# Token combinations of the first large block on VectorE instead of GpSimd, one per row tile, in an attention kernel with two feed-forward layers

## Chip, cores and metric

One core of a Trainium2 chip runs the whole program. The metric is device microseconds of one execution. A value is the median of several runs.

## What is computed

An attention over 4 x 8 heads of 576 tokens (a local one and one on tokens averaged by four) gives 2304 tokens of 512 features. Two feed-forward layers follow:

```python
def _moe_ref(x, w_in, w_out, s, b):
    h = x @ w_in                  # 512 -> 2048
    r = np.maximum(h, 0.0)
    g = s * (r * r) + b
    return (g @ w_out)            # 2048 -> 512

def _moe2_ref(x, w_in, w_out):
    h = x @ w_in
    g = h - np.tanh(h)
    return (g @ w_out)
```

All is fp32. The kernel splits each matrix operand into a rounded high part and a low part (names ending in h and l) and adds three products: high by high, high by low, low by high.

## The kernel before, in words

The second layer works on blocks of tokens, `SIZES2 = (256, 512, 512, 512, 512)`. The first, of 256 tokens, is the **plain block**. The other four are taken in two pairs, the **large blocks** (`k_` is 0 and 1), by seven products in place of eight (`wino`): sums and differences of weight pieces (`A11`, `S2`, ...) are multiplied by sums and differences of token pieces (`B11`, `T1`, `T2`, `B21`, `T3`, `T4`, `B22`).

The plain block runs over 16 **row tiles** `i`. Each has 12 matmuls for `x @ w_in` (`l1`, into the PSUM tile `ph`, two buffers), then `act2`: tanh on ScalarE into `th`, a difference on VectorE, a rounding cast to `gh` on ScalarE, and the rest `gl` on VectorE, which frees `ph`. Two tiles later come six matmuls for `g @ w_out` (`l2_2`, into `acc`). In between, the last weights are made from raw words (`w_split`: `wraw` to `wf` to `w`, on ScalarE and VectorE; `sf` are sums of weight pieces), and the tokens of the first large block are prepared: `x_load` fetches four pieces into `xr`; `x_ops` makes four differences (`comb`, the **combinations** T1 to T4) and splits all seven pieces into `xo` (`split`: cast on ScalarE, rest `xol` on GpSimd); `w1_split` rounds the first weights of the large block into `w1r`. Then `wino` begins: its products go to PSUM tiles `wb`, first with `w1r`, and later rows of `g` meet weights from the ring `w2r`. `wb` takes the PSUM buffers of `ph`, so the first ones wait for the last `gl`.

The order on each engine comes from a list scheduler at the end of the program (`list_schedule`). Of the instructions that are ready by its own estimates it takes the one of lowest priority number, and numbers rise in the order in which the code is written. `ahead(n)` lowers the number by n. Each engine then works strictly in its order, waiting at every instruction until its inputs and its buffer are there.

In `x_ops` the engine is an argument; for the first pair it is GpSimd, for the second VectorE:

```python
    XENG = (pool, dve)
    ...
            todo = x_ops(XENG[0])
        if i == 9:
            x_place()
            for f in todo:
                f()
```

Of the kernel before, what the change touches and what calls it, by code (L numbers as in the profile page):

```python
# [7 lines left out]
F32 = mybir.dt.float32  # L8
F32R = mybir.dt.float32r
I32, U32, U16 = mybir.dt.int32, mybir.dt.uint32, mybir.dt.uint16  # L10
AF = mybir.ActivationFunctionType
ALU = mybir.AluOpType
# [9 lines left out]
W2_RING = 5  # L22
NB2 = 12
Y0_AT = 6
KC = DM // 128
NF = DFF // 128
NP = NF // 2
# [55 lines left out]
def attention_moe_moe_kernel(ctx: ExitStack, tc, q, k, v, w_in, w_out, s_in, b_in, w2_in, w2_out, out):  # L83
    nc = tc.nc
    pe, act, dve, pool, sp = nc.tensor, nc.scalar, nc.vector, nc.gpsimd, nc.sync
# [12 lines left out]
    d_b = [dram.tile([128, 1024], F32, tag=f"db{i}", name="keep_b") for i in range(NB2)]  # L98
    ydram = [dram.tile([128, KC, NB1], F32, tag=f"y{u}", name=f"y{u}") for u in range(NU)]

    @contextmanager
    def ahead(n):

        tc.cur_priority = tc.cur_priority - n
        yield
        tc.cur_priority = tc.cur_priority + n
# [4 lines left out]
    scal = sb.tile([128, 2], F32, name="scal")  # L111
    bcol = sb.tile([128, KC], F32, name="bcol")

# [30 lines left out]
    def x_tiles(u):  # L144
        n = u if u < 2 else (u + 1) % 2
        X[u] = [x_p.tile([128, KC, NB1], F32R, tag=f"{t}{n}", name=t) for t in ("xh", "xl")]

# [619 lines left out]
    def l1(ph, p_, xh, xl, i):  # L767
        g, c = i // 4, (i % 4) * 128
        n = 0
        for kc in range(KC):  # L770
            w_h, w_l = wh[ph, "A", g, kc][:, c:c + 128], wl[ph, "A", g, kc][:, c:c + 128]
            x_h, x_l = (xh[kc], xl[kc]) if ph else (xh[:, kc], xl[:, kc])
            for w_, x_ in ((w_h, x_h), (w_h, x_l), (w_l, x_h)):
                pe.matmul(p_, w_, x_, start=n == 0, stop=n == 3 * KC - 1)  # L774
                n += 1
# [80 lines left out]
    def w2_step(slot):  # L856
        while w2s["n"] < NW and w2s["n"] / W2_RATE <= slot:
            n = w2s["n"]
            w_load(1, n)
            w_split(1, n)  # L860
            w2s["n"] += 1
# [83 lines left out]
    def place(items, a, b, how):  # L945
        for n, l_ in enumerate(how(items, b - a)):
            at[a + n] += l_
# [13 lines left out]
    for s_, (n, u, i) in enumerate(seq):  # L961
# [10 lines left out]
        p_ = ps_ph.tile([128, NB1], F32, tag="ph", name="ph")  # L972
# [14 lines left out]
        if s_ == HA - 1:  # L987
# [4 lines left out]
            raw_p = st1.enter_context(tc.tile_pool(name="raw", bufs=2, reuse_waits="tile"))  # L992
        if u == NU - 1 and i == Y0_AT:
            y0.append(fin.tile([128, KC, SIZES2[0]], F32, tag="yf", name="yf"))
            for e in range(2):
# [8 lines left out]
    evac1(NU - 1, None)  # L1004


    XENG = (pool, dve)

    def place(n, shape, dt, name):
        return fin.tile(shape, dt, tag=f"w{n}", name=name) if n < NFIN else sb.tile(shape, dt, tag=f"w{n - NFIN}", name=name)  # L1010
# [11 lines left out]
    def act2(i, p_):  # L1022
        t = fin2.tile([128, SIZES2[0]], F32, tag="th", name="th")
        gh = g_p.tile([128, SIZES2[0]], F32R, tag="gh", name="gh")
        gl = g_p.tile([128, SIZES2[0]], F32R, tag="gl", name="gl")
        act.activation(out=t, in_=p_, func=AF.Tanh)
        dve.tensor_tensor(out=p_, in0=p_, in1=t, op=ALU.subtract)
        act.copy(out=gh, in_=p_)
        dve.tensor_tensor(out=gl, in0=p_, in1=gh.bitcast(F32), op=ALU.subtract)
        gt[0, i] = (gh, gl)  # L1030

    def l2_2(j, i, w_, ts=None):
        gh, gl = gt[j, i]
        w_h, w_l = w_
        for t in range(SIZES2[j] // 128) if ts is None else ts:
            a_, l_ = gh[:, 128 * t:128 * t + 128], gl[:, 128 * t:128 * t + 128]
            for n, (g_, x_) in enumerate(((a_, w_h), (a_, w_l), (l_, w_h))):
                pe.matmul(accs[j][t], g_, x_, start=i == 0 and n == 0, stop=i == NF - 1 and n == 2)  # L1038
# [26 lines left out]
    ost = {}  # L1065
    w1f = []
    xo, xr, w1r, w2r, tmp, gT = {}, {}, {}, {}, {}, {}
    XOPS = ("B11", "T1", "T2", "B21", "T4", "T3", "B22")
    RAWS = ("B11", "B12", "B22", "B21", "T1", "T2", "T3", "T4")
    AT_X = (*range(40, 44), *range(10))  # L1070

    def x_place():
        for n, o in enumerate(XOPS):
            xo[o] = [place(AT_X[2 * n + i], [128, 2, 512], F32R, "xo" + "hl"[i]) for i in range(2)]

    def x_load(k_):
        for n, o in enumerate(RAWS):
            xr[o] = place(32 + n, [128, 2, 512], F32, "xr")
        for o, j, e in (("B11", 0, 0), ("B12", 1, 0), ("B22", 1, 1), ("B21", 0, 1)):
            load_y(1 + 2 * k_ + j, e, xr[o])  # L1080

    def x_ops(eng):
        def comb(o, a, b):
            return lambda: eng.tensor_tensor(out=xr[o], in0=xr[a], in1=xr[b], op=ALU.subtract)

        def split(o):
            def f():
                h, l = xo[o]
                act.copy(out=h, in_=xr[o])
                eng.tensor_tensor(out=l, in0=xr[o], in1=h.bitcast(F32), op=ALU.subtract)  # L1090
            return f
        return [comb("T1", "B12", "B11"), split("B11"), comb("T2", "B22", "T1"), split("T1"), comb("T4", "B21", "T2"),
                split("T2"), split("B21"), comb("T3", "B22", "B12"), split("T4"), split("T3"), split("B22")]

    def w1_place():
        for q_ in range(2):
            w1r[q_] = [place(32 + 4 * q_ + n, [128, 2, 512], F32R, "w1r") for n in range(4)]

    def w1_load(q_):
        if q_ >= 2 * NP:  # L1100
            return
        if not w1f:
            w1f.extend(place(10 + n, [128, 2, 512], F32, "w1f") for n in range(2))
        g, a = q_ % NP // 2, q_ % 2
        for c in range(2):
            sp.dma_start(out=w1f[0][:, c], in_=d_a[g, c, a])
            sp.dma_start(out=w1f[1][:, c], in_=d_s[g, c][a])

    def w1_split(q_):
        t = w1r[q_ % 2]  # L1110
        for n in range(2):
            act.copy(out=t[2 * n], in_=w1f[n])  # L1112
            dve.tensor_tensor(out=t[2 * n + 1], in0=w1f[n], in1=t[2 * n].bitcast(F32), op=ALU.subtract)
# [8 lines left out]
    def w2_place():  # L1122
        for n in range(W2_RING):
            w2r[n] = place(12 + n, [128, 1024], F32R, "w2r")

    def w2_fetch(m):
        if m < 4 * NB2:
            sp.dma_start(out=w2r[m % W2_RING].bitcast(F32), in_=d_b[m % NB2])
# [77 lines left out]
    def l2_row(j, i, ts=None):  # L1206
        l2_2(j, i, w2_use(j, i), ts)
        if ts is None or ts[-1] == 3:
            if i < NB2:
                w2_fetch(NB2 * (j - 1) + i + W2_RING)  # L1210
# [4 lines left out]
    for i in range(NF):  # L1215
        p_ = ps_ph.tile([128, SIZES2[0]], F32, tag="ph", name="ph2")
        l1(1, p_, ys[0], ys[1], i)
        act2(i, p_)
        if i >= LAG:
            l2_2(0, i - LAG, w_b(i - LAG))  # L1220
        w2_step(NF * NU + i - W2_SLOT0)
        if i == 0:
            x_load(0)
            todo = x_ops(XENG[0])
        if i == 9:
            x_place()
            for f in todo:
                f()
            w1_load(0)
            w1_place()  # L1230
            for q_ in range(2):
                w1_split(q_)
                w1_load(q_ + 1)
        if i == 13:
            w2_place()
            for n in range(W2_RING):
                w2_fetch(n)
    tmp_place()

    for k_ in range(2):  # L1240
        j = 1 + 2 * k_
        for p_ in range(NP):
            def fill(n):
                if p_:
                    l2_row(j, 2 * p_ - 2 + min(n, 1), (None, [0, 1], [2, 3])[n])
                elif n < 2:
                    if k_:
                        l2_row(j - 1, NF - 2 + n)
                    else:
                        l2_2(0, NF - 2 + n, w_b(NF - 2 + n))  # L1250
                else:
                    evac2(j - 1)
                    accs[j] = banks(k_ == 0)
            wino(k_, p_, fill)
        for i in range(2):
            cast(j + 1, i, gT[i // 2][:, i % 2])
            l2_row(j, NF - 2 + i)
        evac2(j)
        accs[j + 1] = banks(k_ == 1)
        if k_ == 0:  # L1260
            x_load(1)
            todo = x_ops(XENG[1])
        for i in range(2, NF):
            cast(j + 1, i, gT[i // 2][:, i % 2])
            l2_row(j + 1, i - 2)
            if k_ == 0:
                for f in todo[3 * i - 6:3 * i - 3]:
                    f()
                if i == 7:
                    w1_place()  # L1270
                    for q_ in range(NP, NP + 2):
                        w1_split(q_)
                        w1_load(q_ + 1)

# [330 lines left out]
```

## Time and profile before

| | |
|---|---|
| median of 3 runs | 963.03 us (962.78 to 963.73) |
| profiled execution | 964.05 us, span of its instructions 962.0 us |
| TensorE busy | 922.8 us, 96% of the span |
| VectorE busy | 731.8 us, 76% |
| ScalarE busy | 504.1 us, 52% |
| GpSimd busy | 181.2 us, 19% |
| mean granted TensorE clock | 0.954 of full |

The span runs from the first to the last instruction; the execution's own time is 2.05 us more. Busy TensorE means that a matmul is in flight, at whichever clock was granted. The plain block begins at 563.8 us of the span.

### The profile page before, as it was taken

To read this page: it belongs to the slowest core of one execution; us is meant where nothing else is said; L and a number is where in the kernel's file an instruction comes from. 1 tells how busy PE (TensorE), PEld (TensorE's weight loads), DVE (VectorE), ACT (ScalarE), POOL (GpSimd) and SP (SyncE) were. 2 spreads that over 40 slices of the span, in tenths; PEclk is the share of its full clock that TensorE was granted. 3 is DMA by queue.
4 is the path that set the end of the run, shared out by engine and by line. 5 is a ranking of instruction groups with operands and counts; after the bars stand their busy time and mean duration, and the time that the engine had idled before them with its cause. 6 is when DMAs were issued, how large, how long until landed. Compare 5 with 4: busy or idle time off the path is not lost.

```text
span 962.0 us, 15484 instructions
## 1 busy us (share of the span) xinstructions
PE 922.8 (96%) x5690; PEld 825.4 (86%) x5690; DVE 731.8 (76%) x1145; ACT 504.1 (52%) x1270; POOL 181.2 (19%) x139
## 2 busy tenths in 40 slices
PE   7999999969999999998999999599999999999998
PEld 6888999959999999998999999478888888888886
DVE  4567899899899999998977785987677737776621
ACT  4679654534746565464676766244434524343321
POOL 1444342432412313232200005600000000000000
PEclk7559999988999999999999999799999999999999
DMA  9991052443123132301159969154354653433061
GB/s 221 307 335 43 26 162 67 130 127 114 37 83 109 61 116 79 98 19 41 47 206 360 366 215 363 73 194 156 110 159 126 221 173 110 166 127 103 24 195 44
DMA packets 82354, 137.38 MB, mean 143 GB/s; under 512 B 23415, under 2 KB 49255, under 8 KB 82279
## 3 DMA queue, kind: packets, MB, share of 16 engines
q1 hardware_dynamic: 80662, 134.04, 42.7%
q10 hardware_dynamic: 1616, 2.36, 0.8%
q8 instruction: 45, 0.74, 0.3%
q14 instruction: 31, 0.25, 0.1%
HBM read 111.66 MB, written 24.71 MB: 142 GB/s over the span
## 4 chain that ended last, share of the span: by engine, by line
PE 74%; DVE 11%; ACT 8%; issue 3%; DMA 2%; SPq 2%; DVEq 0%; ACTq 0%
PE acc L1038 19%; PE ph L774 17%; PE wb L1179 15%; PE acc L807 14%; ACT pA L253 2%; PE S L583 2%; DVE s L194 2%; DVE xq L322 1%; PE O L606 1%; DVE pD L189 1%; SPq L510 1%; ACT E L409 1%; PE warm L892 1%; DVE gl L795 1%; DVE O L265 1%
## 5 line engine op out<-in xcount | busy, mean ns | idle before, releaser
L774 PE MATMUL ph<-xh,w 128*128 128x288 f32 x1024 | 235.5, 304 | 2.5 <-DVE gl L795 1.9
L807 PE MATMUL acc<-gh,w 128*128 128x288 f32 (+1 forms) x1024 | 227.7, 298 | 1.5 <-DVE yst L830 0.9
L774 PEld LDWEIGHTS ph<-xh,w 128*128 128x128 f32 x1024 | 174.2, 192 | 8.8 <-DVE gl L795 3.8
L807 PEld LDWEIGHTS acc<-gh,w 128*128 128x128 f32 x1024 | 171.4, 189 | 3.0 <-issue 1.7
L774 PE MATMUL ph<-xl,w 128*128 128x288 f32 x512 | 154.4, 302 | 0.1
L807 PE MATMUL acc<-gl,w 128*128 128x288 f32 x512 | 151.3, 296 | 0.7 <-DVE gl L795 0.7
L1179 PE MATMUL wb<-xoh,w1r 128*128 128x512 f32 x448 | 147.9, 395 | 0.7 <-ACT w1r L1112 0.7
L1038 PE MATMUL acc<-w2r,gx 128*128 128x512 f32 x576 | 137.2, 390 | 0.0
L1038 PEld LDWEIGHTS acc<-w2r,gx 128*128 128x128 f32 x576 | 108.1, 188 | 23.3
L786 ACT ACTIVATE ph<-ph 128x288 f32<-128x288 f32 x128 | 50.9, 398 | 105.5 <-PE ph L774 102.1
L1179 PEld LDWEIGHTS wb<-xoh,w1r 128*128 128x128 f32 x448 | 84.4, 189 | 21.3 <-ACT w1r L1112 1.1
L774 PEld LDWEIGHTS ph<-xl,w 128*128 128x128 f32 x512 | 98.0, 191 | 1.4 <-issue 0.6
L807 PEld LDWEIGHTS acc<-gl,w 128*128 128x128 f32 x512 | 96.7, 189 | 1.5 <-DVE gl L795 0.9
L1179 PE MATMUL wb<-xol,w1r 128*128 128x512 f32 x224 | 88.6, 395 | 0.0
L795 DVE TENSOR_TENSOR gl<-ph,gh 128x288 fp32r<-128x288 f32 x128 | 57.8, 452 | 29.8 <-ACT gh L792 28.9
L253 ACT ACTIVATE pA<-V,a 128x64 f32<-128x64 f32 x198 | 54.0, 342 | 9.8 <-DVE a L242 6.1
L1173 DVE TENSOR_TENSOR u<-wb,u 128x512 f32<-128x512 f32 x64 | 43.9, 687 | 15.7 <-PE wb L1179 15.7
L792 ACT CAST gh<-ph 128x288 fp32r<-128x288 f32 x128 | 50.8, 398 | 6.3 <-PE acc L807 3.1
L752 DVE SCALAR_TENSOR_TENSOR wf<-wraw 128x512 int32<-128x512 int32 x64 | 50.2, 799 | 3.7 <-ACT wraw L706 2.9
L787 ACT ACTIVATE ph<-ph 128x288 f32<-128x288 f32 x128 | 50.9, 398 | 2.4
L1165 DVE TENSOR_TENSOR gx<-gT,gx 128x512 fp32r<-128x512 f32 x32 | 22.1, 690 | 38.8 <-ACT gx L1164 38.6
L1179 PEld LDWEIGHTS wb<-xol,w1r 128*128 128x128 f32 x224 | 42.2, 189 | 9.8
(169 smaller groups left out, 1602.0 us busy)
## 6 DMA issues: line engine op xcount, KB each, us to landing
w2r<-keep_b SPq DMA_DIRECT2D x48, 512.0 KB
wraw<-in_moe_w_in_dram SPq DMA_DIRECT2D x32, 512.0 KB
wraw<-in_moe_w_out_dram SPq DMA_DIRECT2D x32, 512.0 KB
w1f<-keep_a SPq DMA_DIRECT2D x32, 256.0 KB
w1f<-keep_s SPq DMA_DIRECT2D x32, 256.0 KB
keep_b<-w SPq DMA_DIRECT2D x12, 512.0 KB
y<-yst SPq DMA_DIRECT2D x36, 144.0 KB
K<-in_k_dram SPq DMA_DIRECT2D x5, 960.0 KB
```

The lines of the kernel that those rows point to most:

```text
L253: act.activation(out=p_[:, t, h], in_=Vt[u][:, h, o + t], func=AF.Copy, scale=st["a"][:, h * TAU + t, o:o + 1])
L752: dve.scalar_tensor_tensor(out=f, in0=hw, scalar=3, in1=lw, op0=ALU.logical_shift_left, op1=ALU.bitwise_or)
L774: pe.matmul(p_, w_, x_, start=n == 0, stop=n == 3 * KC - 1)
L786: act.activation(out=p_, in_=p_, func=AF.Relu)
L787: act.activation(out=p_, in_=p_, func=AF.Square)
L792: act.copy(out=gh[:, :NB1], in_=p_)
L795: dve.tensor_tensor(out=gl, in0=p_, in1=gh[:, :NB1].bitcast(F32), op=ALU.subtract)
L807: pe.matmul(accs[u][e][:, :g_.shape[1]], w_, g_, start=i == first and n == 0, stop=i == last and n == 2)
L1038: pe.matmul(accs[j][t], g_, x_, start=i == 0 and n == 0, stop=i == NF - 1 and n == 2)
L1165: dve.tensor_tensor(out=t[:, 1], in0=g_, in1=t[:, 0].bitcast(F32), op=ALU.subtract)
L1173: add = lambda o, x, y: dve.tensor_tensor(out=o, in0=x, in1=y, op=ALU.add)
L1179: pe.matmul(b_, w1_op(q_, o, kc, i), xo[x][m][:, kc], start=n == 0, stop=n == 5)
```

## The change

The eleven elementwise operations that GpSimd did for the first large block (four combinations, seven rests `xol`) are given to VectorE. They are no longer written all at row tile 9 but one per tile from tile 5 (`X_AT`) on. The order of T3 and T4 changes, the buffers of `xr` are numbered so that the first half of `w1r` needs only four of the pieces to be used up, and each half of `w1r` is placed and written separately. `act2` of the plain block is written with a priority that is 60 ahead.

```diff
+P_ACT2 = 60
...
-    XENG = (pool, dve)
+    X_AT = 5
...
-    XOPS = ("B11", "T1", "T2", "B21", "T4", "T3", "B22")
-    RAWS = ("B11", "B12", "B22", "B21", "T1", "T2", "T3", "T4")
+    XOPS = ("B11", "T1", "T2", "B21", "T3", "T4", "B22")
+    RAWS = ("B11", "B12", "T1", "T2", "B22", "B21", "T3", "T4")
...
-    def x_ops(eng):
+    def x_ops():
         def comb(o, a, b):
-            return lambda: eng.tensor_tensor(out=xr[o], in0=xr[a], in1=xr[b], op=ALU.subtract)
+            return lambda: dve.tensor_tensor(out=xr[o], in0=xr[a], in1=xr[b], op=ALU.subtract)
...
                 act.copy(out=h, in_=xr[o])
-                eng.tensor_tensor(out=l, in0=xr[o], in1=h.bitcast(F32), op=ALU.subtract)
+                dve.tensor_tensor(out=l, in0=xr[o], in1=h.bitcast(F32), op=ALU.subtract)
             return f
-        return [comb("T1", "B12", "B11"), split("B11"), comb("T2", "B22", "T1"), split("T1"), comb("T4", "B21", "T2"),
-                split("T2"), split("B21"), comb("T3", "B22", "B12"), split("T4"), split("T3"), split("B22")]
+        return [comb("T1", "B12", "B11"), split("B11"), comb("T3", "B22", "B12"), comb("T2", "B22", "T1"), split("T1"),
+                comb("T4", "B21", "T2"), split("T2"), split("B21"), split("T3"), split("T4"), split("B22")]
...
-        act2(i, p_)
+        with ahead(P_ACT2):
+            act2(i, p_)
...
-            todo = x_ops(XENG[0])
-        if i == 9:
-            x_place()
-            for f in todo:
+            todo = x_ops()
+        if i >= X_AT:
+            for f in todo[i - X_AT:i - X_AT + 1]:
                 f()
+        if i == X_AT + 7:
             w1_load(0)
-            w1_place()
-            for q_ in range(2):
-                w1_split(q_)
-                w1_load(q_ + 1)
+            w1_place(0)
+            w1_split(0)
+            w1_load(1)
+        if i == min(X_AT + 11, NF - 1):
+            w1_place(1)
+            w1_split(1)
+            w1_load(2)
```

GpSimd's list loses its last eleven instructions and nothing else; it has no work left in the second layer. How the scheduler's order moves is seen at two places. On VectorE, behind the weight sums `sf_7174` of row tile 8, before (`ph2` and `gl` numbered 7560, 7648 and 7674 are tiles 9, 10 and 11; `wraw_7342` is the first of the last four raw weights):

```order
L732 TENSOR_TENSOR sf_7174<-wf_7128,sf_7174 128x2x128
L1027 TENSOR_TENSOR ph2_7560<-ph2_7560,th_7573 128x256
L1029 TENSOR_TENSOR gl_7575<-ph2_7560,gh_7574 128x256
L1027 TENSOR_TENSOR ph2_7648<-ph2_7648,th_7661 128x256
L708 TENSOR_SCALAR wraw_7342<-wraw_7342 128x512
L1029 TENSOR_TENSOR gl_7663<-ph2_7648,gh_7662 128x256
L752 SCALAR_TENSOR_TENSOR wf_7346<-wraw_7342 128x512
```

and now (tiles 9, 10 and 11 are 7567, 7597 and 7624):

```order
L733 TENSOR_TENSOR sf_7174<-wf_7128,sf_7174 128x2x128
L1090 TENSOR_TENSOR xol_7510<-xr_7302,xoh_7509 128x1024
L1028 TENSOR_TENSOR ph2_7567<-ph2_7567,th_7580 128x256
L1081 TENSOR_TENSOR xr_7304<-xr_7303,xr_7302 128x1024
L1030 TENSOR_TENSOR gl_7582<-ph2_7567,gh_7581 128x256
L1081 TENSOR_TENSOR xr_7308<-xr_7306,xr_7303 128x1024
L1028 TENSOR_TENSOR ph2_7597<-ph2_7597,th_7610 128x256
L1081 TENSOR_TENSOR xr_7305<-xr_7306,xr_7304 128x1024
L1030 TENSOR_TENSOR gl_7612<-ph2_7597,gh_7611 128x256
L1090 TENSOR_TENSOR xol_7594<-xr_7304,xoh_7593 128x1024
L1028 TENSOR_TENSOR ph2_7624<-ph2_7624,th_7637 128x256
L709 TENSOR_SCALAR wraw_7342<-wraw_7342 128x512
```

One combination or rest stands between every two steps of the row tiles, from tile 9 on.

The second place is where the plain block passes into the large one. On ScalarE, before (`gh_7776` and `gh_7802` are tiles 14 and 15, `w1r_7624` is the first high part of `w1r`):

```order
L1026 ACTIVATE th_7775<-ph2_7762 128x256
L706 ACTIVATE wraw_7447<-wraw_7447 128x512
L1089 CAST xoh_7594<-xr_7309 128x1024
L1028 CAST gh_7776<-ph2_7762 128x256
L1112 CAST w1r_7624<-w1f_7618 128x1024
L1026 ACTIVATE th_7801<-ph2_7788 128x256
L757 CAST w_7453<-wf_7451 128x512
L1028 CAST gh_7802<-ph2_7788 128x256
```

and now (tiles 14 and 15 are 7756 and 7786, `w1r_7690` and `w1r_7692` the high parts of the first half of `w1r`):

```order
L1027 ACTIVATE th_7755<-ph2_7742 128x256
L758 CAST w_7418<-wf_7416 128x512
L1111 CAST w1r_7690<-w1f_7684 128x1024
L758 CAST w_7453<-wf_7451 128x512
L1029 CAST gh_7756<-ph2_7742 128x256
L1111 CAST w1r_7692<-w1f_7685 128x1024
L1027 ACTIVATE th_7785<-ph2_7772 128x256
L1029 CAST gh_7786<-ph2_7772 128x256
```

The cast `gh` of tile 14 now stands behind three casts of weights, where a step on raw weights and one cast of tokens stood. On VectorE, before, from the last row tile's difference on:

```order
L1027 TENSOR_TENSOR ph2_7788<-ph2_7788,th_7801 128x256
L760 TENSOR_TENSOR w_7453<-wf_7451,w_7453 128x512
L1029 TENSOR_TENSOR gl_7803<-ph2_7788,gh_7802 128x256
L1113 TENSOR_TENSOR w1r_7625<-w1f_7618,w1r_7624 128x1024
L1050 COPY ost_7903<-acc_7265 128x512
```

and now, from tile 14's on:

```order
L1028 TENSOR_TENSOR ph2_7742<-ph2_7742,th_7755 128x256
L761 TENSOR_TENSOR w_7418<-wf_7416,w_7418 128x512
L1090 TENSOR_TENSOR xol_7681<-xr_7307,xoh_7680 128x1024
L761 TENSOR_TENSOR w_7453<-wf_7451,w_7453 128x512
L1030 TENSOR_TENSOR gl_7757<-ph2_7742,gh_7756 128x256
L1112 TENSOR_TENSOR w1r_7691<-w1f_7684,w1r_7690 128x1024
L1028 TENSOR_TENSOR ph2_7772<-ph2_7772,th_7785 128x256
L1112 TENSOR_TENSOR w1r_7693<-w1f_7685,w1r_7692 128x1024
L1030 TENSOR_TENSOR gl_7787<-ph2_7772,gh_7786 128x256
L1090 TENSOR_TENSOR xol_7729<-xr_7308,xoh_7728 128x1024
L1172 TENSOR_TENSOR u2_7815<-wb_7828,p1_7814 128x512
```

Two weight rests and one token rest now stand ahead of the `gl` of tile 14 and two rests of `w1r` ahead of that of tile 15; three token rests follow behind it, the fourth a little later. Before, the token rests were GpSimd's and the rests of `w1r` came after the last `gl`. On TensorE the order is the same up to row tile 12; the same 192 + 96 + 60 matmuls of the plain block and of `wb` stand ahead of the first one with `w2r` in both programs.

## Rows read from the trace of the kernel before

**Rows 1.** The page: span, and the granted clock in 40 slices (24.05 us each).

```profile
span 962.0 us, 15484 instructions
...
PEclk7559999988999999999999999799999999999999
```

**Rows 2.** Windows: stretch, its length, each engine's busy time, clock, DMA share, GB/s.

```profile
588.70:603.00 14.30, 14.30 (x94) 12.90 (x93) 7.61 (x13) 10.10 (x18) 14.24 (x6) 1.00 1.04 404
...
604.79:630.00 25.21, 13.11 (x45) 10.07 (x46) 19.77 (x20) 8.46 (x15) 11.88 (x5) 0.73 0.20 72
...
640.67:962.00 321.33, 317.08 (x1381) 258.50 (x1379) 200.78 (x276) 120.13 (x179) 0.00 (x0) 1.00 0.41 134
```

**Rows 3.** Timeline of TensorE: start, duration, instruction, [idle before <-releaser].

```profile
587.67 0.28 PE L774 MATMUL ph<-yxh,w 128*128 128x256 f32 x1
...
590.50 0.28 PE L774 MATMUL ph<-yxh,w 128*128 128x256 f32 x1
...
610.71 1.22 PE L1038 MATMUL acc<-w,gh 128*128 128x512 f32 x2 [5.93 <-ACT gh L1028]
...
622.55 2.07 PE L1038 MATMUL acc<-w,gh 128*128 128x512 f32 x4 [5.49 <-ACT gh L1028]
...
629.40 0.50 PE L1179 MATMUL wb<-xoh,w1r 128*128 128x512 f32 x1 [0.68 <-ACT w1r L1112]
...
630.20 0.40 PE L1179 MATMUL wb<-xol,w1r 128*128 128x512 f32 x1
...
630.90 0.62 PE L1179 MATMUL wb<-xoh,w1r 128*128 128x512 f32 x2
...
640.67 2.90 PE L1038 MATMUL acc<-w2r,gx 128*128 128x512 f32 x12
```

**Rows 4.** Timeline of ScalarE.

```profile
607.06 0.58 ACT L757 CAST w<-wf 128x512 fp32r<-128x512 f32 x1 [5.54 <-DVE wf L752]
...
628.30 2.00 ACT L1112 CAST w1r<-w1f 128x1024 fp32r<-128x1024 f32 x2
```

**Rows 5.** Timeline of VectorE in the plain block.

```profile
588.24 0.42 DVE L732 TENSOR_TENSOR sf<-wf,sf 128x256 f32<-128x256 f32 x1
...
600.33 0.42 DVE L1029 TENSOR_TENSOR gl<-ph,gh 128x256 fp32r<-128x256 f32 x1 [0.73 <-ACT gh L1028]
600.67 3.46 DVE L708 TENSOR_SCALAR wraw<-wraw 128x512 int32<-128x512 int32 x2
604.05 5.72 DVE L752 SCALAR_TENSOR_TENSOR wf<-wraw 128x512 int32<-128x512 int32 x2
...
613.09 4.70 DVE L732 TENSOR_TENSOR sf<-wf 128x256 f32<-128x256 f32 x2
```

**Rows 6.** Timeline of GpSimd.

```profile
588.76 2.41 POOL L1090 TENSOR_TENSOR xol<-xr,xoh 128x1024 fp32r<-128x1024 f32 x1 [111.25 <-DMA xr<-y]
...
598.89 2.40 POOL L1090 TENSOR_TENSOR xol<-xr,xoh 128x1024 fp32r<-128x1024 f32 x1
...
603.80 5.40 POOL L1090 TENSOR_TENSOR xol<-xr,xoh 128x1024 fp32r<-128x1024 f32 x2
612.52 7.46 POOL L1090 TENSOR_TENSOR xol<-xr,xoh 128x1024 fp32r<-128x1024 f32 x3 [3.31 <-ACT xoh L1089]
```

**Rows 7.** Timeline of VectorE in the second pair's preparation.

```profile
752.77 1.22 DVE L1084 TENSOR_TENSOR xr<-xr 128x1024 f32<-128x1024 f32 x1
753.91 0.69 DVE L1165 TENSOR_TENSOR gx<-gT,gx 128x512 fp32r<-128x512 f32 x1
754.51 1.22 DVE L1090 TENSOR_TENSOR xol<-xr,xoh 128x1024 fp32r<-128x1024 f32 x1
...
789.96 0.69 DVE L1173 TENSOR_TENSOR u<-wb,p 128x512 f32<-128x512 f32 x1 [6.92 <-PE wb L1179]
```

**Rows 8.** TensorE's timeline and a window behind an earlier, shorter wait.

```profile
436.25 0.31 PE L435 MATMUL PT<-ident,E 72*72 72x72 f32 x1 [2.53 <-DVE E L423]
...
436.20:439.00 2.80, 2.75 (x13) 2.72 (x14) 2.80 (x5) 1.19 (x3) 1.49 (x1) 0.50 0.83 249
```

More of the change, by code (lines that the diff above doesn't have):

```diff
@@ L1067, in attention_moe_moe_kernel @@
     xo, xr, w1r, w2r, tmp, gT = {}, {}, {}, {}, {}, {}
-    XOPS = ("B11", "T1", "T2", "B21", "T4", "T3", "B22")
-    RAWS = ("B11", "B12", "B22", "B21", "T1", "T2", "T3", "T4")
+    XOPS = ("B11", "T1", "T2", "B21", "T3", "T4", "B22")
+    RAWS = ("B11", "B12", "T1", "T2", "B22", "B21", "T3", "T4")
     AT_X = (*range(40, 44), *range(10))
-    def x_place():
-        for n, o in enumerate(XOPS):
-            xo[o] = [place(AT_X[2 * n + i], [128, 2, 512], F32R, "xo" + "hl"[i]) for i in range(2)]
     def x_load(k_):
@@ L1080, in x_load, with w1_place @@
             load_y(1 + 2 * k_ + j, e, xr[o])
-    def x_ops(eng):
+    def x_ops():
         def comb(o, a, b):
-            return lambda: eng.tensor_tensor(out=xr[o], in0=xr[a], in1=xr[b], op=ALU.subtract)
+            return lambda: dve.tensor_tensor(out=xr[o], in0=xr[a], in1=xr[b], op=ALU.subtract)
         def split(o):
             def f():
+                if o not in xo:
+                    n = 2 * XOPS.index(o)
+                    xo[o] = [place(AT_X[n + i], [128, 2, 512], F32R, "xo" + "hl"[i]) for i in range(2)]
                 h, l = xo[o]
                 act.copy(out=h, in_=xr[o])
-                eng.tensor_tensor(out=l, in0=xr[o], in1=h.bitcast(F32), op=ALU.subtract)
+                dve.tensor_tensor(out=l, in0=xr[o], in1=h.bitcast(F32), op=ALU.subtract)
             return f
-        return [comb("T1", "B12", "B11"), split("B11"), comb("T2", "B22", "T1"), split("T1"), comb("T4", "B21", "T2"),
-                split("T2"), split("B21"), comb("T3", "B22", "B12"), split("T4"), split("T3"), split("B22")]
-    def w1_place():
-        for q_ in range(2):
-            w1r[q_] = [place(32 + 4 * q_ + n, [128, 2, 512], F32R, "w1r") for n in range(4)]
+        return [comb("T1", "B12", "B11"), split("B11"), comb("T3", "B22", "B12"), comb("T2", "B22", "T1"), split("T1"),
+                comb("T4", "B21", "T2"), split("T2"), split("B21"), split("T3"), split("T4"), split("B22")]
+    def w1_place(q_):
+        w1r[q_] = [place(32 + 4 * q_ + n, [128, 2, 512], F32R, "w1r") for n in range(4)]
     def w1_load(q_):
@@ L1223, in attention_moe_moe_kernel @@
             x_load(0)
-            todo = x_ops(XENG[0])
-        if i == 9:
-            x_place()
-            for f in todo:
+            todo = x_ops()
+        if i >= X_AT:
+            for f in todo[i - X_AT:i - X_AT + 1]:
                 f()
+        if i == X_AT + 7:
             w1_load(0)
-            w1_place()
-            for q_ in range(2):
-                w1_split(q_)
-                w1_load(q_ + 1)
+            w1_place(0)
[5 more added lines that the diff above has]
+            w1_load(2)
         if i == 13:
@@ L1261, in attention_moe_moe_kernel @@
             x_load(1)
-            todo = x_ops(XENG[1])
+            todo = x_ops()
         for i in range(2, NF):
@@ L1269, in attention_moe_moe_kernel @@
                 if i == 7:
-                    w1_place()
                     for q_ in range(NP, NP + 2):
+                        w1_place(q_ % 2)
                         w1_split(q_)
```

## Prediction

> **What bounds the kernel now.** I read the page first, for the stretches where TensorE is not at full clock: of its 40 slices the one from 601 to 625 us shows 7 tenths, in a kernel that is otherwise at 9 nearly throughout behind the start [rows 1]. Then windows around that place. TensorE is busy for all of 588.7 to 603, but for only 13.1 of the 25.2 us from 604.8 to 630, and there at 0.73 of the clock; from 640.7 to the end it is busy for 317 of 321 us at clock 1.00 [rows 2]. So a stall between 604 and 630 is on the path, and what is won there is carried to the end unshortened.
>
> TensorE's timeline names the stall: waits of 5.93, 5.49 and 0.68 us for casts of ScalarE, 12.1 us in all [rows 3]. ScalarE was not the cause: it had itself waited 5.54 us for the `wf` of VectorE [rows 4]. VectorE was busy all that time, but with what should be short: two operations of line 708 took 3.46 us and two of line 752 took 5.72, and later two sums of line 732 took 4.70, while the `gl` at 600.33, which reads PSUM, took its 0.42 [rows 5]. A sum of line 732 at 588.24, ahead of GpSimd's first operation, took 0.42 too. What is present only in the long cases is GpSimd, at work on the token pieces from 588.76 on, 2.4 to 2.7 us for each operation [rows 6], also over that `gl`: VectorE's operations that read SBUF alone wait for it, the row tile's steps stand behind them in VectorE's order, ScalarE waits for those, and TensorE for ScalarE.
>
> **The term that is removed.** I count the TensorE work from the first matmul of row tile 9 (587.67) to the first one with `w2r` (640.67), which both programs reach after the same matmuls. A row tile of 12 + 6 matmuls takes 590.50 - 587.67 = 2.83 us [rows 3]. Seven of them (tiles 9 to 15, with the `l2` of 7 to 13) are 19.8 us. Twelve matmuls of `l2` (tiles 14, 15) and 60 of `wb` remain; three start-to-start steps of `wb` from 630.20 to 630.90 give 0.233 us each [rows 3], so 72 are 16.8 us. Together 36.6, and without any stall the `w2r` row would start at 624.3. It starts at 640.67, so 16.4 us are lost: 12.1 in waits and, by difference, 4.3 to the lower clock behind them. That is the most that the change can win in this stretch.
>
> **The term that is added.** Eleven operations of 128 x 1024 come to VectorE. Its own rows for the second pair, where GpSimd has nothing to do, give their price: 1.22 us, and 752.77 to 753.91, that is 1.14 from start to start, for a combination; a rest `xol` has the same 1.22 [rows 7]. So 12.5 us of VectorE, in a stretch where it was busy 7.6 of 14.3 us before [rows 2]; GpSimd's shared time no longer lengthens the rest. The question is when VectorE is through with what TensorE needs at the hand-over. I add up its new order from 588.66 (the end of the sum at 588.24) with start-to-start steps: 0.34 for an operation of 0.42 (600.33 to 600.67) [rows 5], 0.60 for one of 0.69 (753.91 to 754.51) [rows 7], 1.14 as above.
>
> - Up to the `wf` of the third of the last four weights: seven token operations (8.0), five differences and five `gl` (3.4), four of line 709 (1.4), three `wf` (1.8), two weight rests (1.2), four sums (1.4): 17.2, so 605.9. ScalarE then has that weight's cast, one of `w1r` and one more weight (0.5 + 1.0 + 0.5, from 0.58 and 2.00 for two [rows 4]) ahead of the `gh` of tile 14, which ends at 608.3. A clean TensorE needs it at 587.67 + 19.8 = 607.5. Gap 0.85.
> - To the `gl` of tile 14: one more `wf`, a difference, two weight rests, one `xol`, the `gl`: 3.6, so 609.5. The first product needs its PSUM buffer; TensorE is there after four matmuls, at 609.25. Gap 0.3.
> - To the `gl` of tile 15: two rests of `w1r`, a difference, the `gl`: 3.0, so 612.5. The third product needs it; TensorE is there at 613.3. No gap.
> - To the second half of `w1r`: three `xol` (3.4), eight steps of the large block (4.8), a rest of `w1r`, a step, a rest (2.9): 623.6. TensorE, late by 1.2 so far, wants the last of these at about 623.3. Gap 0.3.
>
> That is 1.5 us if VectorE never waits for ScalarE and a release costs nothing. It can only be more; for these waits I add 0.9, and take 2.4. The bounds: 0 at one end (some of the gaps close if an estimate is a little high), and at the other the waits that the same steps show when they miss each other, treated as a rival below.
>
> Other edits. The priority of `act2` and the order T3, T4 act through the orders summed above and cost nothing of their own. The same matmuls, casts and transfers are issued; SyncE's list differs only from the refills of `w1f` on, which come earlier with the rests that free them. In the second pair the preparation is written in the new order too; there the `wino` stage that it feeds shows VectorE idle for 6.92 us, waiting for TensorE, before its first step at 789.96 [rows 7], more than 30 us behind the combinations, so a shift of a few operations stays hidden. Without that cover a late piece would cost TensorE its lateness, a few times 1.14 us.
>
> **Sum.** 16.4 - 2.4 = 14.0 us less. The profiled execution took 964.05 us, 2.05 more than its span of 962.0; less 14.0 that is 950.0. It stands 1.0 above the median of the runs, so the median should be 963.0 - 14.0 = **949.0**.
>
> **A rule against the change.** The trace shows VectorE with idle time before 603 and, by the sum above, with none from there to the hand-over. The Trainium skill (Perfetto Trace Analysis, Optimizing Scalar/DVE Operations) says that with VectorE saturated, moving work to ScalarE or even GpSimd may pay, and warns that VectorE and GpSimd share an SBUF read port, so a move between those two might not. Its first half makes the first rival of what follows, and the sum by it would be that rival's; its warning is what the rows of 3.46 and 5.72 us look like.
>
> **Rivals.**
>
> *VectorE becomes the bound at the hand-over.* The gaps add up, and one grows long. For it: the sum leaves VectorE no slack from 603 to 623. Against it: the steps that TensorE waits for have priority, and by the count its largest gap is 0.85. Price: a wait of 2.53 us elsewhere left the matmuls at half the clock over 436.2 to 439.0 and to about 439.4 [rows 8], some 3.2 us at half rate, 1.6 lost. With such a gap (2.5 + 1.6) beside my 2.4 the new loss is 6.5, the gain 9.9, the time 953.1.
>
> *The low clock stays, and the kernel is slower.* If TensorE drops to 1.2 GHz at the first gap and the small gaps keep it there up to the `w2r` row, the 21.3 us of clean work left at 603 take twice as long: 21.3 + 2.4 = 23.7 lost against 16.4 now, so 7.3 slower, 970.3. It decides from (16.4 - 2.4) / 21.3, about two thirds of that work at the low clock. For it: behind an earlier stall the page shows 8 tenths over two slices, 192 to 241 us [rows 1]. Against it: from 630 on, right behind the worst stalls, the clock is 1.00 at once.
>
> *Nothing is won, since another wait ends last.* A transfer or a ScalarE cast could hold the same matmuls to the old times. Against it: none of the three waits of TensorE names a transfer [rows 3], and over the worst stretch the transfers took a share of 0.20 [rows 2]. Within 0.2% (some 2 us, about what a measurement of this kernel can tell from no change) it would need a new wait of 12 us and more.
>
> **How the numbers follow.** The forecast has 0.74, VectorE as the bound 0.20, the persistent clock 0.03, no change 0.03. The forecast's own range goes from 946.6 (no new gap: 963.0 - 16.4) to 951. To take in most of the first rival I go to 954; below, half a microsecond for the counting: 946 to 954. Faster by over 0.2%: 0.94, within: 0.03, slower: 0.03.
>
> **What the new profile would show.** GpSimd without work behind the attention. Lines 709, 753 and 733 at 0.42, 0.69 and 0.42 us in every row. Combinations and rests on VectorE at 1.22. TensorE without a wait above 1 us between 588 and 630 and at clock 1.00 or close to it; the first `w2r` matmul near 626.7. After that point everything as before, 14 us earlier. I am wrong if one of the waits at the hand-over is longer than 2 us, if TensorE's clock is low for more than a few us there, or if VectorE's operations keep their long durations without GpSimd.

## The result and the profile after

The changed kernel takes 947.40 us (median of 4 runs, 947.06 to 948.10); the kernel before took 963.38 beside it (962.78 to 966.64). The ratio is 0.9828, 95% interval 0.9805 to 0.9851. The forecast was 949.0 with a range of 946 to 954: faster, and inside the range, 1.6 us below the forecast.

The page of the kernel after answers to [rows 1]. The slice that had 7 tenths of the clock, the 26th, is at 9. GpSimd, busy for 181.2 us before and 155.0 now, shows zeros behind the middle.

```profile
span 945.7 us, 15470 instructions
...
PE 918.5 (97%) x5690; PEld 822.7 (87%) x5690; DVE 730.3 (77%) x1156; ACT 504.1 (53%) x1270; POOL 155.0 (16%) x128
...
POOL 1544343341411413133100000000000000000000
PEclk7559999997999999999999999999999999999999
```

The windows that answer to [rows 2] follow (stretch, length, busy time of PE, PEld, DVE, ACT and POOL, clock, DMA share, GB/s). TensorE is busy for 24.86 of 25.21 us from 604.8 to 630, where it had 13.11 at clock 0.73, and the clock is 1.00. VectorE is busy for all of the first window and 24.66 of the second: as forecast, it has no slack. The last window begins just ahead of the first `w2r` matmul.

```profile
588.70:603.00 14.30, 14.30 (x88) 12.39 (x87) 14.30 (x24) 11.20 (x20) 0.00 (x0) 1.00 1.04 404
604.79:630.00 25.21, 24.86 (x114) 19.93 (x113) 24.66 (x35) 13.75 (x21) 0.00 (x0) 1.00 0.54 165
624.00:945.70 321.70, 317.48 (x1384) 259.11 (x1382) 201.55 (x278) 121.88 (x180) 0.00 (x0) 1.00 0.42 135
```

TensorE's timeline answers to [rows 3]. The first matmul of tile 9 starts at 587.35 (587.67 before), and in place of the waits of 5.93, 5.49 and 0.68 us there is a single one of 0.35, for the `gh` of tile 14. The first product `wb` starts at 608.91 without one, the first `w2r` matmul at 624.70 (640.67 before).

```profile
587.35 0.28 PE L775 MATMUL ph<-yxh,w 128*128 128x256 f32 x1
...
607.12 0.40 PE L1039 MATMUL acc<-w,gl 128*128 128x512 f32 x1
607.87 1.20 PE L1039 MATMUL acc<-w,gh 128*128 128x512 f32 x4 [0.35 <-ACT gh L1029]
608.91 0.42 PE L1178 MATMUL wb<-xoh,w1r 128*128 128x512 f32 x1
...
624.70 2.90 PE L1039 MATMUL acc<-w2r,gx 128*128 128x512 f32 x12
```

VectorE's timeline answers to [rows 5] and [rows 7]. Line 709 (708 before) takes 0.75 for two where it took 3.46, line 753 takes 1.29 for two where it took 5.72. A token operation takes 1.21 to 1.23.

```profile
588.39 1.23 DVE L1090 TENSOR_TENSOR xol<-xr,xoh 128x1024 fp32r<-128x1024 f32 x1
589.54 0.42 DVE L1028 TENSOR_TENSOR ph<-ph,th 128x256 f32<-128x256 f32 x1
589.87 1.22 DVE L1081 TENSOR_TENSOR xr<-xr 128x1024 f32<-128x1024 f32 x1
...
604.08 0.75 DVE L709 TENSOR_SCALAR wraw<-wraw 128x512 int32<-128x512 int32 x2
604.75 1.29 DVE L753 SCALAR_TENSOR_TENSOR wf<-wraw 128x512 int32<-128x512 int32 x2
...
608.62 0.41 DVE L1030 TENSOR_TENSOR gl<-ph,gh 128x256 fp32r<-128x256 f32 x1
...
611.55 0.41 DVE L1030 TENSOR_TENSOR gl<-ph,gh 128x256 fp32r<-128x256 f32 x1
...
621.93 1.21 DVE L1112 TENSOR_TENSOR w1r<-w1f,w1r 128x1024 fp32r<-128x1024 f32 x1
```

The span is 16.3 us shorter: 0.32 ahead of tile 9, 53.00 - 37.35 = 15.65 from there to the `w2r` row, and 0.33 behind it.

### The profile page after: what moved, and what is told of

Same layout as the page of the kernel before. It is cut to its first block, busy times and chain, and to the rows that moved or that the text cites. A ratio compares the mean times of both kernels' runs of the same rounds, so it can differ in the third digit from the quotient of the medians.

```text
span 945.7 us, 15470 instructions
## 1 busy us (share of the span) xinstructions
PE 918.5 (97%) x5690; PEld 822.7 (87%) x5690; DVE 730.3 (77%) x1156; ACT 504.1 (53%) x1270; POOL 155.0 (16%) x128
## 4 chain that ended last, share of the span: by engine, by line
PE 77%; DVE 10%; ACT 8%; issue 3%; SPq 1%; DMA 1%; DVEq 0%; ACTq 0%
PE acc L1039 20%; PE ph L775 18%; PE wb L1178 16%; PE acc L808 14%; ACT pA L254 2%; PE S L584 2%; DVE s L195 2%; DVE xq L323 1%; DVE pD L190 1%; PE O L607 1%; DVE O L266 1%; SPq L511 1%; ACT E L410 1%; PE warm L893 1%; DVE gl L796 1%
## 5 line engine op out<-in xcount | busy, mean ns | idle before, releaser
L362 DVE TENSOR_REDUCE pp<-raw 72x256 f32<-72x1024 f32 x24 | 48.6, 2028 | 0.4 <-DMA raw<-in_q_dram 0.4
```

What stands on the lines that cost most here:

```text
L362: dve.tensor_reduce(out=t2.rearrange("p a h d -> p (a h) d").unsqueeze(3), in_=t[:GH].rearrange("p a h r d -> p (a h) d r"), axis=AX, op=A ...
```

## Experiments

All times are medians; the kernel before took 962.6 to 963.4 beside them. The theory is that of the prediction: GpSimd at work on SBUF lengthens VectorE's operations there, and TensorE waits at the end of that chain. Two questions are open after the result: is the contention enough, and is the new order of any worth, since the prediction only summed it up?

| token operations on | written | `act2` | us | ratio, 95% interval |
|---|---|---|---|---|
| GpSimd | all at tile 9 | plain (before) | 963.4 | 1 |
| GpSimd | all at tile 9 | 60 ahead | 963.2 | 0.9996 [0.9982, 1.0010] |
| GpSimd | one per tile | 60 ahead | 962.0 | 0.9986 [0.9969, 1.0004] |
| VectorE | all at tile 9 | plain | 958.4 | 0.9947 [0.9928, 0.9967] |
| VectorE | all at tile 9 | 60 ahead | 952.0 | 0.9900 [0.9873, 0.9926] |
| VectorE | one per tile | plain | 949.4 | 0.9879 [0.9846, 0.9912] |
| VectorE | one per tile | 60 ahead (after) | 947.4 | 0.9828 [0.9805, 0.9851] |

The rows "one per tile" have the new buffer numbers, the new order of T3 and T4 and the split `w1r` too; of these only the buffer numbers were tried by themselves.

**The new order with GpSimd** (the kernel after, `x_ops` with the engine as an argument again; the two calls are shown):

```diff
-            todo = x_ops()
+            todo = x_ops(pool)
...
-            todo = x_ops()
+            todo = x_ops(dve)
```

> The changed kernel with only the engine put back: the eleven token operations of the first pair on GpSimd again, still one per row tile and with the priority of act2 kept. Theory (what was won is VectorE's time behind GpSimd): operations of lines 709, 753 and 733 take 2 to 3 us again while GpSimd works, TensorE waits 8 us or more between 600 and 630, time 958 to 966. Rival (the spreading, the placing and the priority are what won): 947 to 949.

961.98 us: spreading and priority by themselves win about 1 us, which can't be told from nothing. On GpSimd, though, the spreading is one of the program text only: its eleven operations run from 587.61 to 618.59 here and from 588.76 to 619.98 in the kernel before [rows 6]. GpSimd's first and last row of this kernel:

```profile
587.61 2.40 POOL L1090 TENSOR_TENSOR xol<-xr,xoh 128x1024 fp32r<-128x1024 f32 x1 [111.39 <-DMA xr<-y]
...
613.59 5.00 POOL L1090 TENSOR_TENSOR xol<-xr,xoh 128x1024 fp32r<-128x1024 f32 x2 [3.30 <-ACT xoh L1089]
```

VectorE's timeline has the long rows again, and TensorE's a wait of 6.91 us behind them:

```profile
600.71 4.62 DVE L709 TENSOR_SCALAR wraw<-wraw 128x512 int32<-128x512 int32 x2
605.25 5.58 DVE L753 SCALAR_TENSOR_TENSOR wf<-wraw 128x512 int32<-128x512 int32 x2
```

```profile
611.78 1.65 PE L1039 MATMUL acc<-w,gh 128*128 128x512 f32 x3 [6.91 <-ACT gh L1029]
```

**The priority alone** (the kernel before):

```diff
-        act2(i, p_)
+        with ahead(60):
+            act2(i, p_)
```

> The kernel before with act2 of the plain block 60 ahead and nothing else: GpSimd keeps all eleven token operations, written at row tile 9. If GpSimd beside VectorE is what holds the passage and the order only matters once VectorE is free of it, the priority cannot shorten the long weight steps on VectorE (L708, L752 and the sums at 4 to 6 us in twos), and the time is 961 to 965 us, within 0.3% of the kernel before. If the priority were an independent gain, as large alone as it is on top of the engine (958.4 to 952.0), it would be 955 to 958 us.

963.16 us, no change. As long as GpSimd holds up the weight steps, the order ahead of them is worth nothing.

**The engine alone** (the kernel before):

```diff
-    XENG = (pool, dve)
+    XENG = (dve, dve)
```

> The kernel before with only the engine changed: the eleven token operations on VectorE, all written at row tile 9, no priority, old placing. Theory: most of the gain, 948 to 953; no long operation on VectorE. Rival (order): TensorE still waits 8 us or more since VectorE's burst stands ahead of the row tiles, 957 to 963.

958.43 us: the theory of 948 to 953 fails here, and the rival holds by its time, though the waits that it put at 8 us or more come to 6.75. No operation of VectorE is long any more, yet TensorE waits 2.69, 1.36 and 2.70 us between 594 and 612. The first of these, in TensorE's timeline:

```profile
597.66 1.20 PE L1038 MATMUL acc<-w,gh 128*128 128x512 f32 x4 [2.69 <-ACT gh L1028]
```

ScalarE's timeline of the same kernel shows four casts of tokens, a raw weight step and a fifth cast in a row, and only then the `th` of the next row tile:

```profile
589.26 2.00 ACT L1089 CAST xoh<-xr 128x1024 fp32r<-128x1024 f32 x2
591.58 2.00 ACT L1089 CAST xoh<-xr 128x1024 fp32r<-128x1024 f32 x2 [0.32 <-DVE xr L1084]
593.48 0.69 ACT L706 ACTIVATE wraw<-wraw 128x512 f32<-128x512 f32 x1
594.05 1.03 ACT L1089 CAST xoh<-xr 128x1024 fp32r<-128x1024 f32 x1
594.99 0.37 ACT L1026 ACTIVATE th<-ph 128x256 f32<-128x256 f32 x1
```

VectorE takes the difference of that tile at 596.14, behind a run of token and weight operations. All of them have their own right length; they stand ahead of a step that TensorE needs. So in this case the same work on VectorE wins a third of the 16 us, and the order the rest.

**The engine and the priority** (both edits above on the kernel before):

> The kernel before with the engine changed and the priority of act2, the token operations still all written at row tile 9 and the old places. Theory: the priority alone gives back most of what the run with the engine alone lacked: 948.5 to 952, what is left being the late first half of w1r. Rival (the operations must be spread over the tiles): 955 to 959.

951.95 us, at the upper end of what the theory gave. With VectorE free of GpSimd, the priority that was worth nothing gives 6.5 us. The longest wait left is not the expected one for the late `w1r`, which is 0.91 us, but one of 1.92 us for the `gl` of a row tile.

**Without the priority** (the kernel after, `P_ACT2 = 0`):

> The changed kernel with the priority of act2 set to 0, all else as changed. Theory now (two terms: VectorE freed of GpSimd is worth some 5 us, the row tiles kept ahead of the token operations the other 11): token operations written at earlier tiles stand ahead of tile 10's steps again, on VectorE two in a row where the changed kernel has one, on ScalarE several casts; TensorE waits 1 to 3 us there, 949 to 954. Rival (the spreading by tiles is what keeps them apart, the priority does nothing): 947 to 948.

949.36 us, 2.0 above the kernel after (the two intervals just overlap), with waits of 1.04, 0.86 and 0.22 us for `gl` and `gh` between 596 and 604. Spreading, with the edits that come with it, does most of what the priority does: on top of the engine it gives 9.1 us by itself and 4.6 behind the priority.

**The old buffer numbers** (the kernel after):

```diff
-    RAWS = ("B11", "B12", "T1", "T2", "B22", "B21", "T3", "T4")
+    RAWS = ("B11", "B12", "B22", "B21", "T1", "T2", "T3", "T4")
```

> The changed kernel with the old numbering of the token pieces' buffers, so that the first half of w1r lies where the last piece to be split (B22) was. Theory: its second rest comes three token rests and a copy later than in the changed kernel, some 5 us, of which TensorE can hide 1 or 2 behind the first products: 949 to 952. Rival (the buffers only shift work on engines with time to spare): 947 to 948.

948.71 us (947.33 to 949.02), ratio 0.9861 [0.9836, 0.9887]. TensorE waits 1.38 us at 614.76 for a `w1r`, and its `w2r` row comes 1.34 us later. The wait is seen, and is smaller than expected; the two times can hardly be told apart.

**Contention without any other change** (the kernel after; ten operations of GpSimd on a tile that nothing reads, from the same time on; the scheduler's estimates leave them out, so that every other engine keeps its order):

```diff
+        if i == X_AT + 1:
...
+            idle = fin.tile([128, 2, 512], F32, tag="yf", name="idle")
+            for n in range(10):
+                pool.tensor_tensor(out=idle, in0=idle if n else xr["B11"], in1=idle if n else xr["B11"], op=ALU.subtract)
...
```

> The changed kernel and, beside it, ten operations of GpSimd with the old shape that read and write a tile nobody uses, started by the first token piece; the orders of all other engines are unchanged. Theory (contention alone, no result is waited for): VectorE's operations with both inputs in SBUF and those of lines 709 and 753 take up to 3 us over some 25 us, TensorE waits, time 958 to 970. Rival (the old loss was that TensorE or VectorE waited for GpSimd's results): 947 to 948.

959.58 us: work that nobody waits for costs 12 us. GpSimd's row, and VectorE's beside it:

```profile
588.79 22.23 POOL L1232 TENSOR_TENSOR idle<-idle 128x1024 f32<-128x1024 f32 x9
```

```profile
593.33 1.78 DVE L733 TENSOR_TENSOR sf<-wf,sf 128x256 f32<-128x256 f32 x1
595.02 2.91 DVE L1090 TENSOR_TENSOR xol<-xr,xoh 128x1024 fp32r<-128x1024 f32 x1
597.86 0.42 DVE L1028 TENSOR_TENSOR ph<-ph,th 128x256 f32<-128x256 f32 x1
...
601.03 2.58 DVE L1081 TENSOR_TENSOR xr<-xr 128x1024 f32<-128x1024 f32 x1
```

A combination takes 2.58 instead of 1.21, a sum 1.78 instead of 0.41; the difference that reads `ph` in PSUM keeps its 0.42. One of GpSimd's nine takes 22.23 / 9 = 2.47 us, so VectorE gets about one two-input operation through for each of GpSimd's. TensorE waits 1.17, 4.61, 1.06 and 2.73 us for `gl`.

That is an average. In the kernel before, with GpSimd busy for 14.24 of the 14.30 us from 588.7 on [rows 2], lines 708 and 752 also had rows of only 0.87 and 0.84 us; what fixes the length of a single one is not shown.

```profile
592.95 0.87 DVE L708 TENSOR_SCALAR wraw<-wraw 128x512 int32<-128x512 int32 x1
...
595.81 0.84 DVE L752 SCALAR_TENSOR_TENSOR wf<-wraw 128x512 int32<-128x512 int32 x1
```

**GpSimd that only writes** (as the last, with one reading operation and 24 memsets in place of the ten):

> As the run with ten idle operations of GpSimd, but one operation that reads and then 24 memsets of the same tile, which only write. Theory with the lock on reading (the Trainium skill, SBUF - State Buffer, Who interferes with whom: two SBUF inputs contend with a GpSimd operation that reads, not with one that only writes): 947 to 949.5, operations with two SBUF inputs at 0.69 and 1.22 us. Rival (any GpSimd work in SBUF slows VectorE): 955 and more.

948.34 us, 0.9 above the kernel after. GpSimd is busy as long, but VectorE's combinations and sums keep their times; only line 709 is longer, 1.09, 0.54 and 1.59 for two, where the kernel after has 0.41, 0.41 and 0.75. TensorE waits 0.29, 0.53 and 1.18 us between 599 and 610.

```profile
586.15 24.95 POOL L1233 MEMSET idle<- 128x1024 f32 x24
```

```profile
589.58 1.22 DVE L1081 TENSOR_TENSOR xr<-xr 128x1024 f32<-128x1024 f32 x1
...
595.44 1.09 DVE L709 TENSOR_SCALAR wraw<-wraw 128x512 int32<-128x512 int32 x1
...
604.57 1.59 DVE L709 TENSOR_SCALAR wraw<-wraw 128x512 int32<-128x512 int32 x2
```

So it is not GpSimd's being busy that costs VectorE its time, but what GpSimd does in SBUF. The Trainium skill (SBUF — State Buffer, Who interferes with whom) states just this: two SBUF inputs on VectorE contend with GpSimd's reads and not with its writes, and `tensor_scalar` may take both shared ports; the two traces agree.

**VectorE with more work** (the kernel after, each of the seven `xol` of the first pair done twice):

```diff
-                dve.tensor_tensor(out=l, in0=xr[o], in1=h.bitcast(F32), op=ALU.subtract)
+                for _ in range(1 + rep):
+                    dve.tensor_tensor(out=l, in0=xr[o], in1=h.bitcast(F32), op=ALU.subtract)
...
-            todo = x_ops()
+            todo = x_ops(1)
```

> The changed kernel with each of the seven token rests of the first pair written twice, 7 x 1.14 = 8.0 us more of VectorE. Theory by the count in the prediction (VectorE has no idle time between 588 and 624, TensorE is within 1 us of waiting for it): about 4.6 us of that lie ahead of the last gl, TensorE ends 5 to 8 us later: 952 to 956. Rival (VectorE has slack that the count does not see): under 949.5.

953.84 us: 8.0 us more on VectorE cost 6.4 at the end. The `w2r` row comes at 632.06, 7.36 later; the longest of six waits of TensorE is for a rest:

```profile
624.60 0.50 PE L1179 MATMUL wb<-xol,w1r 128*128 128x512 f32 x1 [2.04 <-DVE xol L1091]
```

**A stretch elsewhere with the same look.** In the kernel after, TensorE's longest wait is now in the attention, 4.94 us at 205.7 (4.93 in the kernel before). It ends with VectorE's sum at 209.13, which has its own length of 1.34. But VectorE is busy throughout, and ahead of that sum in its order, with four operations between, stands another that took 3.32 us beside a product of GpSimd, where the same kind of sum took 1.35 just before. So the long sum can account for 2.0 us of the wait, and the rest is work that stands ahead of the last sum in VectorE's order; the expectations below take the long sum for the one that TensorE waits for. TensorE, VectorE and GpSimd there, one timeline each of the kernel after:

```profile
210.62 1.82 PE L305 MATMUL xt<-ident,O 128*128 128x128 f32 x8 [4.94 <-DVE O L266]
```

```profile
200.10 1.35 DVE L266 TENSOR_TENSOR O<-O,pP 128x1152 f32<-128x1152 f32 x1
...
202.64 3.32 DVE L266 TENSOR_TENSOR O<-O,pA 128x1152 f32<-128x1152 f32 x1
...
209.13 1.34 DVE L266 TENSOR_TENSOR O<-O,pP 128x1152 f32<-128x1152 f32 x1
```

```profile
201.53 3.21 POOL L258 TENSOR_TENSOR pP<-V,a 128x1152 f32<-128x1152 f32 x1 [9.42 <-DVE O L266]
```

Two kernels move one and both of that unit's value products from GpSimd to VectorE (`PV_POOL2 = (4,)` and `()` in place of `(4, 6)`).

> The kernel after, with one of the two value products of attention unit 2 on VectorE instead of GpSimd. In the kernel after, TensorE waits 4.94 us at 205.7 us for a sum O of VectorE that took 3.32 us in place of 1.35 beside a GpSimd product of 3.21 us, and the granted clock falls behind it. If that overlap is what makes the wait, it goes, and the time is 943 to 946 us; VectorE's extra product costs 1.3 us. If VectorE's own amount of work bounds that stretch, the wait stays or grows and the time is 947 to 950 us.

> The kernel after, with both value products of attention unit 2 on VectorE. If contention makes the 4.94 us wait, 943 to 946 us, as with one product moved or 1 us better. If VectorE's own work is the bound there, two products of 1.3 us are added to it and the time is 948 to 951 us.

With one moved, 946.13 us (943.52 to 949.19): just above the 943 to 946 of the theory, and not to be told from the kernel after. A wait of 2.96 us up to the same 210.62 is left. With both, 943.90 us (940.32 to 944.81), ratio 0.9796 [0.9771, 0.9822]: better than before and, by its four runs, all below the four of the kernel after, though the two intervals overlap a little. The long sum is gone, the wait for `O` too, and the windows below (the kernel after, then this one) show 25.39 us of TensorE in place of 21.09.

```profile
195.00:225.00 30.00, 21.09 (x120) 17.93 (x119) 29.45 (x41) 10.62 (x29) 11.93 (x5) 0.77 0.38 121
```

```profile
195.00:225.00 30.00, 25.39 (x155) 22.45 (x154) 27.06 (x47) 12.61 (x35) 7.41 (x3) 0.83 0.35 112
```

The 948 to 951 us that VectorE's own work as the bound would have given did not come. That the gain comes from this place is not shown, since the move shifts the order of the whole attention. With both products moved the transposes `xt` behind this wait start 3.81 us earlier than in the kernel after (206.81), the next ones 2.89 later (268.95 for 266.06), and the first `w2r` row 2.85 earlier (621.85). And another wait of TensorE in the kernel after is gone in both traces:

```profile
436.03 0.30 PE L436 MATMUL PT<-ident,E 72*72 72x72 f32 x1 [2.53 <-DVE E L424]
```

## Why the prediction was right, step by step

- **What bounds the kernel, and the cause.** Right. The long operations are gone [rows 5], and idle GpSimd operations that read and write SBUF bring them back in an unchanged order, at 12 us, while ones that only write cost next to nothing (0.9).
- **The term removed, 16.4 us.** Right. 36.6 us of clean work from 587.35 would bring the `w2r` row to 623.95; it comes at 624.70. The 12.1 us of waits and the 4.3 of low clock are both gone: 15.65 us won and 0.75 newly lost make 16.4.
- **The term added, 2.4 us: the one that was mis-sized.** The new loss is 0.75, less than the 1.5 that were counted, so "it can only be more" was wrong and the 0.9 that I added for waits on ScalarE was not needed. VectorE came to each step of the count about half a microsecond earlier than forecast: third `wf` 605.44 (605.9 forecast; the end of the first of the two in the row at 604.75), `gl` of tile 14 at 609.03 (609.5), `gl` of tile 15 at 611.96 (612.5), second half of `w1r` 623.14 (623.6). Its chain starts 0.27 us earlier than I took, with the row at 588.39. At the `gh` of tile 14 TensorE is 0.7 us late (607.87 for 587.35 + 19.8), where 0.85 was forecast. The row's wait of 0.35 is less than that because idle time is counted from the end of a matmul of 0.40 us, while matmuls start every 0.233: from start to start the gap is 607.87 - 607.12 - 0.233 = 0.52, and 0.2 was lost over the tiles before. At the first product 0.1 is added (the four `acc` matmuls at 607.87 take 1.04 to the next start, where four steps of 0.233 are 0.93), where 0.3 was forecast, and the 0.3 at `w1r` did not come. Where several operations miss each other by 0.3 us, half a microsecond of start decides.
- **The priority and the order "cost nothing of their own".** True, but a poor account of them. The count was made along the new order, and was right for that reason; it left unsaid that the priced work in the old order wins 5 us and not 14. The runs put the worth of the order at 11 us with VectorE free of GpSimd and, without, at about 1, which can't be told from nothing.
- **VectorE as the bound (0.20, 953.1).** Not so, but near: with doubled rests it happens, at 953.8, and with one long wait of 2.04 as pictured. The kernel after stands at the edge of it.
- **The low clock (0.03) and no change (0.03).** The clock is 1.00 through the hand-over, and no transfer takes the waits' place.
- **Sum.** 14.0 us less were forecast; the medians give 16.0, the spans 16.3. The 2.3 between forecast and span are 1.65 of new gaps that were not there, and 0.32 and 0.33 ahead of and behind the stretch, whose cause stays open and which no term of the prediction stood for.
- **The rule on saturated engines.** By the page of the Trainium skill that the prediction weighed (Perfetto Trace Analysis, Optimizing Scalar/DVE Operations) a saturated VectorE would speak for GpSimd. Here VectorE is saturated at 24.66 of 25.21 us and still the better place; the page's own warning about the shared port is what decides, as the two kernels with idle work show.

## What to carry to other kernels

When a few VectorE operations take four to six times what their kind takes elsewhere, look at what GpSimd reads in SBUF meanwhile; moving its share to VectorE may cost less than VectorE loses. Price the move along the order in which it will run, since the right engine in a bad order gave a third of the gain here and the edits of the order with the work left on GpSimd next to none. Look afterwards for the same look in the other stages: here a second place gave perhaps 3 us more, and how it came about is not shown.

## What was not expected of the hardware

Beside GpSimd's memsets of 1.04 us, VectorE's line 709 (`TENSOR_SCALAR`, int32, 128 x 512) went from 0.41 to 1.09 us, while line 753 with its two SBUF inputs stayed at 0.69. Beside GpSimd's operations that read, both lines are long, 2.31 and 2.79 us for one in the kernel with the new order on GpSimd. And TensorE kept clock 1.00 over a wait of 0.35 us; in the engine-alone kernel TensorE is idle for 4.05 us of the window below, and the granted clock is 0.88.

```profile
588.70:603.00 14.30, 10.25 (x56) 8.77 (x55) 14.30 (x25) 10.58 (x17) 0.00 (x0) 0.88 1.04 406
```
